# Attention and two feed-forward blocks on one core: where the moving operands of the matrix products begin in memory

## The chip, the core and the metric

The kernel runs on one core of one Trainium2 chip. The core has a matrix engine (TensorE, PE in the profile), a vector engine (DVE), an activation engine (ACT), GpSimd (POOL) and a queue engine (SP) that starts the transfers. All of them work on one on-chip memory of 128 partitions; an address in this text is a byte offset inside a partition, the same in all 128. The metric is the device time in microseconds of one execution; of three timed executions the median counts.

A matrix product on TensorE has two operands. The stationary one is loaded ahead (LDWEIGHTS, PEld in the profile), 128 columns here. The moving one is streamed past it (MATMUL), 448 or 384 columns of four bytes here.

## What is computed

The reference is a causal attention over 2 batches, 12 heads, 448 positions and 64 values a head, followed by two feed-forward blocks on the 896 tokens:

```
scores = scale * q @ k.T, masked above the diagonal
attn   = softmax(scores);  x = attn @ v             -> [896, 768]
x      = (silu(x @ w_gate) * (x @ w_val)) @ w_out    # 768 -> 1536 -> 768
h      = x @ w_in                                    # 768 -> 2048
out    = (h * clip(h + 3, 0, 6) / 6) @ w_out         # 2048 -> 768
```

## The kernel before

Every product of the two blocks is made three times at a reduced matrix type (fp32r, four bytes a value) from a value cut in two parts, high and low: high by high, high by low and low by high. So each operand is a pair of tiles, and the function `three` or `mm3_parts` issues three MATMULs for one product. Two levels of the block products are combined so that seven block products do the work of eight (`seven` and the stages after it).

The work falls into four stretches. Up to about 85 us is the attention with its transposes (`tp`, `tr`), scores (`sc`) and value products (`pv`). From there to about 429 us come the products whose moving operand has 448 columns: first layer (`x,ws`, `x,a`, `x,s`, `t,a`, `t,s`), output layer (`go,wo`, and `g8` to `g11` with `whi` and `wlo`), and the third matrix (`x,a`, `x,s` again). In the last 115 us the roles are swapped: the weights move (384 columns) and the token values are stationary; first with the gated values `h0` to `h5` as they lie (`whi` or `wlo` by `h..`), then with small tiles made for it (`op`, `tp`, `wo`).

A planner (class `Plan`) writes out the order of all instructions from a list of operations, their costs and their due times, and that order is kept. Nothing in it depends on an address.

What matters here is where the tiles lie. A "place" is a fixed stretch of the partition that a sequence of tiles uses in turn. There are 19 places in the pool `xpool` and 25 more in `ypool`. They hold tiles of [128, 2, 448] or [128, 896] four-byte values, 3,584 bytes, of either kind: plain float32 intermediates, which begin at the place's first byte, and operands of type fp32r. For the second kind the function `moving` (line 303, called from `last` at line 684 and `spot` at line 848) takes a tile of `2 * S + 8` values, 3,616 bytes, and uses the 896 values from the fourth on (`ODD = 3`), so that they begin 12 bytes into the place. The second half of such a tile (the low part, or the second batch) begins 1,792 bytes, seven times 256, after the first.

The stationary operands of the 448-column products, and both operands `op` and `wo` of the last stretch, lie in other pools: eight tiles called `ws` in `ring`, which lies ahead of `xpool`, and a ninth in `more`, which lies behind it. They begin at their first byte.

In the program as it is built, `ring` begins at byte 16,640, and every `ws` tile in it at a multiple of 256. `xpool` begins at byte 59,648, a multiple of 256 too, and its places follow one another every 3,616 bytes (3,584 where a place never holds an operand). 3,616 is 14 times 256 plus 32. So the moving operands begin 12, 44, 76, 108, 140, 172, 204 or 236 bytes past a multiple of 256, some at each. The ninth `ws` tile begins 32 bytes past a multiple of 256. The text calls this remainder, the first byte modulo 256, the offset of an operand.

```
def moving(pool_, tag, shape, name):                                    # L303
    t = pool_.tile([128, 2 * S + 8], F32R, tag=tag, name=name)[:, ODD : ODD + 2 * S]
    return t if len(shape) == 2 else t.rearrange("p (a b) -> p a b", a=2)
def spot(place, shape, dt, name):                                       # L845
    if dt == F32R and shape in ([128, 2, S], [128, NT]):
        return Spot(lambda: moving(pool_, tag, shape, name), place)
```

Of the kernel before, what the change touches and what calls it, by code (L numbers as in the profile page):

```python
# [8 lines left out]
F32 = mybir.dt.float32  # L9
BF16 = mybir.dt.bfloat16  # L10
F32R = mybir.dt.float32r
# [46 lines left out]
AT_START = {"act": 2.0, "vec": 1.3, "pool": 2.0, "pe": 1.2, "sp": 0.3}  # L58
GROUPS = ((2,), (0, 1), (3,))
IDLE = (6, 1, 3, 4)  # L60
ODD = 3
SHARED = ("vec", "pool")


# [26 lines left out]
class Plan:  # L91
# [6 lines left out]
    def op(self, where, call, reads=(), writes=(), port=False, wire=0.0, soon=None, kind=None, by=None):  # L98

        i, before, ready = len(self.ops), set(), 0.0  # L100
        for writing, spots in ((False, reads), (True, writes)):
            for s in spots:
                spot, part = s if isinstance(s, tuple) else (s, None)
                if spot not in self.uses:
                    self.uses[spot] = []
                    old = self.on_place.get(spot.place)
                    if old is not None:
                        spot.after = {j for _, j, _ in self.uses[old]}
                    if spot.place is not None:
                        self.on_place[spot.place] = spot  # L110
                before |= spot.after
                ready = max(ready, spot.ready)
                one = spot.place is not None and spot.place[0] is self.alone
                for p, j, w in self.uses[spot]:
                    if (w or writing or one) and (p is None or part is None or p == part):
                        before.add(j)
                self.uses[spot].append((part, i, writing))
        before.discard(i)
        self.ops.append((where, call, before, ready, port, wire + LANDING if wire else 0.0))
        self.soon.append(soon)  # L120
        self.kinds.append(kind)
        self.by.append(by)
# [93 lines left out]
def tile_attention_glu_mlp(  # L216
# [21 lines left out]
    B, H, S, D = q.shape  # L238
    NT, DM = out.shape
# [21 lines left out]
    consts = const.tile([128, 32], F32, name="half")  # L261
    half, floor = consts[:, :16], consts[:, 16:]
    ring = ctx.enter_context(tc.tile_pool(name="ring", bufs=1))
    xpool = ctx.enter_context(tc.tile_pool(name="xpool", bufs=1))
    banks = ctx.enter_context(tc.tile_pool(name="banks", bufs=1, space=PSUM))

# [32 lines left out]
    more = []  # L299
    lent = {}  # L300
    HD = KD // 2

    def moving(pool_, tag, shape, name):  # L303
        t = pool_.tile([128, 2 * S + 8], F32R, tag=tag, name=name)[:, ODD : ODD + 2 * S]
        return t if len(shape) == 2 else t.rearrange("p (a b) -> p a b", a=2)

    def pair_tile(name, dt=F32R):
        return slot([128, 2, S], dt, name)
# [26 lines left out]
    def attention():  # L335
        with ExitStack() as st:
# [13 lines left out]
            for i in range(NV):  # L350
                t = fix.tile([C, 2, NC, D + 16], F32, name=f"v1_{i}")
# [6 lines left out]
            def take(kind, n, shape, dt=F32, ready=0.0):  # L358

                i = count[kind] = count.get(kind, -1) + 1  # L360
                tag = f"{kind}{i % n}"
                return Spot(lambda: wk.tile(shape, dt, tag=tag, name=kind), (wk, tag), ready=ready)

            def bank(use):
                n = idle.pop(0)
                return Spot(lambda: banks.tile([128, 512], F32, tag=f"bank{n}", name=use), (banks, n)), n
# [263 lines left out]
            def pv_parts(p):  # L630

                if p < 0 or p >= NPAIR:
                    return []
                b, hp = pairs[p]
                vt, ets, sm = v_of[p], et_of.pop(p), s_of.pop(p)
                box = {}

                def product(kc):
                    if kc == 0:
                        box["o"], box["n"] = bank("pv")  # L640
                    o, w = box["o"], (NC - kc) * C

                    def work(eng):
                        for j, et in enumerate(ets):
                            eng.matmul(
                                o()[64 * j : 64 * j + 64, kc * C : S], vt()[:, j, kc, :D], et()[:, KOFF[kc] : KOFF[kc] + w],
                                start=(kc == 0), stop=(kc == NC - 1),
                            )

                    op({"pe": w * 0.0018}, work, reads=[(et, kc) for et in ets] + [vt], writes=[o], kind="pv")  # L650

                def shares():
                    r, rb = take("r", 2, [C, 2, NC]), take("rb", 1, [C, NC, 2, D])
                    tr, bn = bank("tr")
                    rs = box["rs"] = take("rs", 1, [128, S])
                    op(
                        {"pool": 0.22},
                        lambda e: e.tensor_scalar(out=r(), in0=sm(), scalar1=EPS, scalar2=None, op0=ALU.add),
                        reads=[sm], writes=[r],
                    )  # L660
                    op({"vec": 0.19}, lambda e: e.reciprocal(out=r(), in_=r()), writes=[r])
                    op(
                        {"pool": 0.72},
                        lambda e: e.tensor_copy(
                            rb(), r().rearrange("p j c -> p c j").unsqueeze(3).to_broadcast([C, NC, 2, D])
                        ),
                        reads=[r], writes=[rb], port=True,
                    )

                    def work(eng):  # L670
                        for c in range(NC):
                            eng.transpose(
                                tr()[:, c * C : (c + 1) * C], rb()[:, c].rearrange("p j d -> p (j d)"), ident[:C, :C]
                            )

                    op({"pe": 0.4}, work, reads=[rb], writes=[tr], kind="tp")
                    op({"act": 0.44}, lambda e: e.copy(rs(), tr()[:, :S]), reads=[tr], writes=[rs])
                    idle.append(bn)

                def last():  # L680
                    o, rs = box["o"], box["rs"]
                    t = sum_of[id((sums if hp < HD else more_sums)[hp % HD][0])]
                    pool_, tag = place = free.pop(0)
                    x = Spot(lambda: moving(pool_, tag, [128, 2, S], f"x{b}{hp}"), place)
                    x1[b][hp] = x
                    op(
                        {"vec": 0.52},
                        lambda e: e.tensor_tensor(out=t()[:, b], in0=o()[:, :S], in1=rs(), op=ALU.mult),
                        reads=[o, rs], writes=[(t, b)],
                    )  # L690
                    idle.append(box["n"])
                    op(
                        {"pool": 0.57, "act": 0.46}, lambda e: move(e, x()[:, 0], t()[:, b]), reads=[(t, b)],
                        writes=[(x, 0)], by=BY_END if p == NPAIR - 1 else None, port=True,
                    )
                    op(
                        {"pool": 1.16, "vec": 0.58},
                        lambda e: e.tensor_tensor(
                            out=x()[:, 1], in0=t()[:, b], in1=x()[:, 0].bitcast(F32), op=ALU.subtract
                        ),  # L700
                        reads=[(t, b), (x, 0)], writes=[(x, 1)], by=BY_END if p == NPAIR - 1 else None, port=True,
                    )
                    if b == 1 and hp < HD:
                        op(
                            {"pool": 1.16, "vec": 0.58},
                            lambda e: e.tensor_tensor(out=t()[:, 0], in0=t()[:, 1], in1=t()[:, 0], op=ALU.subtract),
                            reads=[(t, 1)], writes=[(t, 0)], port=True,
                        )

                return [lambda kc=kc: product(kc) for kc in range(2)] + [shares] + [  # L710
                    lambda kc=kc: product(kc) for kc in range(2, NC)
                ] + [last]
# [120 lines left out]
    def mlps():  # L833
# [10 lines left out]

        def spot(place, shape, dt, name):  # L845
            pool_, tag = place
            if dt == F32R and shape in ([128, 2, S], [128, NT]):
                return Spot(lambda: moving(pool_, tag, shape, name), place)
            return Spot(lambda: pool_.tile(shape, dt, tag=tag, name=name), place)

        def here(tile_and_place, ready=0.0):
# [199 lines left out]
        for h in range(HD):  # L1051
# [5 lines left out]
            for k, src in ((1, f1), (3, f3), (2, f2), (4, f4)):  # L1057
                t = take([128, 2, S], F32R, f"t{k}{h}")
# [415 lines left out]
        for eh in range(2):  # L1474
# [7 lines left out]
            for t in range(TT):  # L1482
# [4 lines left out]
                if eh == 0:  # L1487
# [3 lines left out]
                    lambda e, t=t, o=parked[t], pt=pt, eh=eh: (e.copy if t % 2 else e.tensor_copy)(  # L1491
                        o()[:, eh], eh_ap(pt())
                    ),
# [36 lines left out]
        x = [bank_spot() for _ in range(HT)]  # L1530
# [111 lines left out]
```

## Time and profile before

| what | value |
|---|---|
| median of 3 runs | 542.26 us (541.87 to 542.31) |
| the profiled execution's own time | 542.55 us |
| its span, first to last instruction | 540.8 us |
| TensorE busy | 534.3 us (99%), 3,099 MATMULs |
| VectorE / ScalarE / GpSimd busy | 455.9 / 418.6 / 146.2 us (84 / 77 / 27%) |
| granted TensorE clock | 1.000 over the span |
| transfers | 69.32 MB, mean 128 GB/s |

MATMULs overlap in the profile: each is shown with its latency, and the next begins before it ends. What a MATMUL adds to the time is the distance from its start to the start of the next one, called its spacing here. Over a run of n MATMULs the spacing is the start of what follows minus the start of the run, divided by n. Where a row of the timeline gives only a run's start and length, the last MATMUL's own length is taken off and the rest divided by n - 1.

### The profile page before, as it was taken

The numbers are of one execution on the slowest core, as the hardware profiler recorded it, in microseconds if no ns is written. First come the engines' busy times: TensorE is split into PE (matmuls) and PEld (weight loads), VectorE is DVE, ScalarE is ACT, GpSimd is POOL, SyncE is SP. The second block draws the span as 40 slices with busy tenths as digits, with TensorE's granted clock in tenths as the row PEclk, the third lists the DMA queues.
The fourth block names the chain that finished last, engine by engine and source line by source line (L and its number), as shares of the span: only waits on it lengthen the run. The fifth ranks groups of instructions, "written<-read, shape, count | busy, mean of one in ns | idle before, by whom it ended". The sixth has DMA issues, their size and how long they took to land.

```text
span 540.8 us, 8943 instructions
## 1 busy us (share of the span) xinstructions
PE 534.3 (99%) x3099; PEld 487.6 (90%) x3099; DVE 455.9 (84%) x931; ACT 418.6 (77%) x877; POOL 146.2 (27%) x163
## 2 busy tenths in 40 slices
PE   8999999999999999999999999999999999999997
PEld 4777777999999999999999999999999999999997
DVE  4999997999878778688998888989888956599982
ACT  5999996878887678588967788899898756686560
POOL 0798988403000000030030143322231300000311
PEclk9999999999999999999999999999999999999999
DMA  7987803355545443332002354465353155510112
GB/s 204 245 215 201 170 17 118 117 180 191 182 148 181 134 135 135 118 116 79 1 1 78 110 176 135 127 185 166 117 163 130 35 180 195 176 58 2 59 45 102
DMA packets 58989, 69.32 MB, mean 128 GB/s; under 512 B 16960, under 2 KB 52544, under 8 KB 58944
## 3 DMA queue, kind: packets, MB, share of 16 engines
q1 hardware_dynamic: 58944, 68.76, 42.4%
q8 instruction: 24, 0.39, 0.3%
q14 instruction: 21, 0.17, 0.1%
HBM read 65.99 MB, written 2.75 MB: 127 GB/s over the span
## 4 chain that ended last, share of the span: by engine, by line
PE 98%; DVE 1%; ACT 0%; issue 0%
PE mm L74 83%; PE pv L74 5%; PE sc L74 4%; PE tp L74 4%; PE tr L74 2%; PE zero L74 1%; DVE out L74 0%; ACT e L74 0%; DVE et L74 0%; ACT qh L74 0%; DVE e L74 0%; DVE zeros L341 0%; DVE half L840 0%; DVE half L839 0%; DVE m L74 0%
## 5 line engine op out<-in xcount | busy, mean ns | idle before, releaser
L74 PE MATMUL mm<-x,a 128*128 128x448 f32 x396 | 85.9, 363 | 0.0
L74 PE MATMUL mm<-x,s 128*128 128x448 f32 x378 | 80.6, 363 | 0.0
L74 PEld LDWEIGHTS mm<-x,a 128*128 128x128 f32 x396 | 74.6, 189 | 5.3
L74 PEld LDWEIGHTS mm<-x,s 128*128 128x128 f32 x378 | 71.2, 188 | 5.1
L74 ACT ACTIVATE raw<-raw,half 128x768 uint32<-128x768 uint8 (+1 forms) x66 | 64.5, 981 | 0.0
L74 PE MATMUL mm<-t,s 128*128 128x448 f32 x270 | 57.8, 363 | 0.0
L74 PE MATMUL mm<-op 128*128 128x384 f32 x315 | 56.5, 336 | 0.0
L74 PEld LDWEIGHTS mm<-op 128*128 128x128 f32 x315 | 55.1, 188 | 0.0
L74 PEld LDWEIGHTS mm<-t,s 128*128 128x128 f32 x270 | 50.7, 188 | 3.7
L74 PE MATMUL mm<-go,wo 128*128 128x448 f32 x252 | 51.2, 363 | 0.0
L74 PEld LDWEIGHTS mm<-go,wo 128*128 128x128 f32 x252 | 47.4, 188 | 3.5 <-issue 0.2
L74 ACT ACTIVATE e<-e,m 112x224 f32<-112x224 f32 (+3 forms) x96 | 49.7, 535 | 0.6 <-DVE m L74 0.6
L74 DVE CUSTOM_DVE_ANT_0 e<-sc,mask 112x224 f32<-112x224 f32 (+3 forms) x96 | 36.6, 440 | 1.2 <-PE sc L74 1.1
L74 DVE SCALAR_TENSOR_TENSOR v<-v,raw 128x768 uint32<-128x768 uint32 x36 | 34.3, 954 | 2.7 <-ACT raw L74 2.4
L74 ACT ACTIVATE w<-raw 128x768 f32<-128x768 f32 (+1 forms) x34 | 29.6, 870 | 8.6 <-DMA raw<-in_moe_w_out_dram 4.3
L74 ACT ACTIVATE v<-raw 128x768 f32<-128x768 f32 x36 | 32.5, 907 | 1.2 <-DMA raw<-in_moe_w_val_dram 1.0
L74 PE MATMUL mm<-x,ws 128*128 128x448 f32 x144 | 30.1, 366 | 0.0
L74 DVE SCALAR_TENSOR_TENSOR w<-w,raw 128x768 uint32<-128x768 uint32 (+1 forms) x30 | 27.2, 906 | 3.0 <-ACT raw L74 3.0
L74 PEld LDWEIGHTS mm<-x,ws 128*128 128x128 f32 x144 | 26.8, 188 | 2.2
L74 ACT COPY tmp<-mm 128x448 f32<-128x448 f32 x40 | 21.2, 532 | 9.0 <-PE mm L74 8.8
L74 ACT CAST op<-h 128x384 fp32r<-128x384 f32 x30 | 15.3, 511 | 16.2 <-PE mm L74 15.5
L74 PE MATMUL tp<-keep,e 112*112 112x112 f32 x240 | 25.8, 260 | 1.4 <-ACT e L74 1.4
(252 smaller groups left out, 1253.6 us busy)
## 6 DMA issues: line engine op xcount, KB each, us to landing
raw<-in_moe_w_out_dram SPq DMA_DIRECT2D x24, 768.0 KB, 4.2
raw<-in_moe_w_in_dram SPq DMA_DIRECT2D x16, 768.0 KB, 4.5
raw<-in_moe_w_gate_dram SPq DMA_DIRECT2D x12, 768.0 KB, 4.2
raw<-in_moe_w_val_dram SPq DMA_DIRECT2D x12, 768.0 KB, 4.2
raw<-in_moe_w_out_dram SPq DMA_DIRECT2D x6, 512.0 KB, 3.4
v<-in_v_dram SPq DMA_DIRECT2D x12, 224.0 KB, 5.1
out_dram<-out SPq DMA_DIRECT2D x14, 192.0 KB, 1.9
nat<-in_k_dram SPq DMA_DIRECT2D x10, 216.0 KB, 4.9
```

The costliest lines, as they stand in the source:

```text
L74: ins = call(*args, **kw)
```

## The change

The function `moving` and the constant `ODD` go. An operand of type fp32r takes a tile of its own size, 3,584 bytes, and begins at the place's first byte, as the plain tiles do. A pool of its own, `front`, with one tile of eight four-byte values (32 bytes) that nothing reads or writes, is put between `ring` and `xpool`.

```
-ODD = 3
+FRONT = 8
...
     ring = ctx.enter_context(tc.tile_pool(name="ring", bufs=1))
+    front = ctx.enter_context(tc.tile_pool(name="front", bufs=1))
+    front.tile([128, FRONT], F32, name="front")
     xpool = ctx.enter_context(tc.tile_pool(name="xpool", bufs=1))
...
-    def moving(pool_, tag, shape, name):
-        t = pool_.tile([128, 2 * S + 8], F32R, tag=tag, name=name)[:, ODD : ODD + 2 * S]
-        return t if len(shape) == 2 else t.rearrange("p (a b) -> p a b", a=2)
-
...
-                    x = Spot(lambda: moving(pool_, tag, [128, 2, S], f"x{b}{hp}"), place)
+                    x = Spot(lambda: pool_.tile([128, 2, S], F32R, tag=tag, name=f"x{b}{hp}"), place)
...
-            if dt == F32R and shape in ([128, 2, S], [128, NT]):
-                return Spot(lambda: moving(pool_, tag, shape, name), place)
             return Spot(lambda: pool_.tile(shape, dt, tag=tag, name=name), place)
```

All five engines have the same instructions in the same order as before; only addresses differ. In the changed program `xpool` begins at byte 59,680 and every place, in `xpool` and `ypool`, is 3,584 bytes (14 times 256) after the one before. All moving operands of the 448-column products therefore have offset 32, and so have the stationary slices of `h0` to `h5`. The `ring` tiles stay at offset 0 and the ninth `ws` tile at offset 32. The attention's own pools move by 512 bytes as a whole, so that their offsets stay, but for the identity matrix of the transposes, which lies in a place of `xpool` and goes from offset 160 to 32.

## Rows read from the trace of the kernel before

**Rows 1.** The page's chain of work that ended last, by engine and line.
```profile
PE 98%; DVE 1%; ACT 0%; issue 0%
```
**Rows 2.** That chain in order of time: start us, us, what.
```profile
92.59 443.01 PE mm L74 x2274
```
**Rows 3.** Waits of PE: engine, line, waited for: us in total, times, longest us.
```profile
PE tp L74 <- ACT e L74: 1.4, 1, 1.4
PE zero L74 <- DVE half L840: 1.2, 1, 1.2
PE sc L74 <- DVE m L74: 0.3, 1, 0.3
```
**Rows 4.** Busy us by stretch: us, PE, PEld, DVE, ACT, POOL, clock, DMA share, GB/s.
```profile
85.00:420.00 335.00, 335.00 (x1681) 311.21 (x1680) 289.43 (x495) 270.77 (x489) 69.76 (x60) 1.00 0.40 128
```
**Rows 5.** MATMUL timeline, output layer: start us, us, operation, count.
```profile
249.12 47.21 PE L74 MATMUL mm<-go,wo 128*128 128x448 f32 x233
```
**Rows 6.** MATMUL timeline, first layer, products of nine.
```profile
118.08 1.98 PE L74 MATMUL mm<-x,a 128*128 128x448 f32 x9
119.90 3.79 PE L74 MATMUL mm<-t,s 128*128 128x448 f32 x18
123.53 1.97 PE L74 MATMUL mm<-x,a 128*128 128x448 f32 x9
125.34 2.03 PE L74 MATMUL mm<-t,s 128*128 128x448 f32 x9
127.21 1.99 PE L74 MATMUL mm<-x,a 128*128 128x448 f32 x9
129.04 2.01 PE L74 MATMUL mm<-t,a 128*128 128x448 f32 x9
130.89 1.98 PE L74 MATMUL mm<-x,s 128*128 128x448 f32 x9
```
**Rows 7.** PE groups by form: operation, count, busy us, mean ns of one, idle.
```profile
L74 PE MATMUL mm<-go,wo 128*128 128x448 f32 x252 | 51.2, 363 | 0.0
L74 PE MATMUL mm<-g11l,whi 128*128 128x448 f32 x12 | 4.4, 367 | 0.0
L74 PE MATMUL mm<-g10h,whi 128*128 128x448 f32 x12 | 4.3, 360 | 0.0
```
**Rows 8.** MATMUL timeline, one round over `h2` to `h5` in the last layer.
```profile
434.56 0.34 PE L74 MATMUL mm<-whi,h2h 128*128 128x384 f32 x1
...
436.49 0.34 PE L74 MATMUL mm<-whi,h5l 128*128 128x384 f32 x1
```
**Rows 9.** By tile: count: duration ns min/median/max, first and last start us.
```profile
L74 PE MATMUL mm<-wlo,h2h x14: 332/332/336, 434.7 to 469.6; 128*128 128x384 f32 x14
...
L74 PE MATMUL mm<-wlo,h3h x14: 339/342/342, 435.3 to 470.1; 128*128 128x384 f32 x14
```
**Rows 10.** MATMUL timeline, last stretch, both operands at a tile's first byte.
```profile
485.68 10.11 PE L74 MATMUL mm<-op 128*128 128x384 f32 x57
495.63 1.21 PE L74 MATMUL mm<-op,tp 128*128 128x384 f32 x6
496.67 3.30 PE L74 MATMUL mm<-op 128*128 128x384 f32 x18
```
**Rows 11.** MATMUL timeline, attention scores, operands at a tile's first byte.
```profile
44.42 0.37 PE L74 MATMUL sc<-kh,qh 64*112 64x448 f32 x2
44.62 0.37 PE L74 MATMUL sc<-kl,qh 64*112 64x448 f32 x2
44.83 0.37 PE L74 MATMUL sc<-kh,ql 64*112 64x448 f32 x2
```
**Rows 12.** DVE and ACT groups by form that write operands or plain tiles.
```profile
L74 DVE TENSOR_TENSOR x<-tmp,x 128x448 fp32r<-128x448 f32 x9 | 5.4, 616 | 0.0
...
L74 DVE TENSOR_TENSOR ts<-g 128x448 f32<-128x448 f32 x4 | 2.5, 615 | 0.0
L74 ACT CAST go<-g 128x448 fp32r<-128x448 f32 x24 | 13.4, 566 | 7.0 <-PE mm L74 6.6
...
L74 ACT CAST qh<-f 128x448 fp32r<-128x448 f32 x3 | 1.7, 564 | 0.0
```
**Rows 13.** By tile, the attention's transposes.
```profile
L74 PE MATMUL tp<-keep,e x240: 257/259/311, 11.2 to 88.7; 112*112 112x112 f32 x120
```

## The prediction, as it was put on record

> **What bounds the kernel now.** I read the chain of work that ended last first: 98% of it is TensorE [rows 1], and from 92.59 us to 535.60 us it is one unbroken piece of 2,274 MATMULs [rows 2]. The waits say the same from the other side: TensorE's waits that have a releaser are three, 2.9 us together, all in the attention or ahead of it [rows 3]. The table by stretch shows why: from 85 to 420 us TensorE is busy for all of 335 us at clock 1.00, while VectorE has 289 us and ScalarE 271 us of work in it and the transfers fill 0.40 of their engines [rows 4]. So the time is a sum of MATMUL spacings. What an instruction of another engine costs matters only if it becomes 14% longer; what a MATMUL costs matters at once: one nanosecond on each 448-column MATMUL is 1.7 us.
>
> How long is the spacing? The run of 233 `go,wo` has a length of 47.21 us, of which the last MATMUL's own 0.36 us is no spacing: 46.85 / 232 = 201.9 ns for 448 columns [rows 5]. I take this for all 1,674 MATMULs with 448 columns (396 `x,a`, 378 `x,s`, 270 `t,s`, 252 `go,wo`, 144 `x,ws`, 90 `t,a`, and 12 groups of 12 with `g8` to `g11`). In the last layer the spacing of 384 columns is 1.93 us / 11 = 175.5 ns while the gated values `h` are stationary [rows 8], and (495.63 - 485.68) / 57 = 174.6 ns with `op` [rows 10].
>
> **Does an address matter at all?** The change moves no instruction; only where operands begin differs. Rows of equal shape that differ by nothing but the place of an operand must answer. They do. The 14 MATMULs of `wlo,h2h` last 332 to 336 ns, the 14 of `wlo,h3h`, one tile on, 339 to 342 ns, in two separate passes [rows 9]: the place decides, not chance. The same holds for the moving side: 360 ns with `g10h` and 367 ns with `g11l` as moving operand [rows 7]. The products of nine in the first layer show it as spacing, and the program tells their offsets. The `x,a` from 123.53 us has its three moving tiles at offsets 12, 44 and 76: (125.34 - 123.53) / 9 = 201.1 ns. The `x,a` from 118.08 and from 127.21 us has them at 172, 204 and 236: 202.2 and 203.3 ns. The `t,a` from 129.04 us has 140, 172 and 204: 205.6 ns [rows 6]. Stationary tiles are at offset 0 in nearly all of them. So there are good offsets and bad ones, some 3 ns apart, and before the change the kernel pays an average over them.
>
> [...]
>
> **The change part by part.** First term: all 1,674 moving operands of 448 columns come to one offset, 32, and begin at the place's first byte. Of this no row shows both together. The nearest offsets that a row shows are 12, 44 and 76, at 201.1 ns [rows 6]. Bounds: below, nothing excludes that the first byte itself costs; the shortest steady spacing of operands that all begin at a tile's first byte is 173.3 ns for 384 columns, (496.67 - 495.63) / 6, against 175.5 ns with a stationary operand 12 bytes further [rows 8, 10]. If 448 columns won the same 2.2 ns, they would have 199.7 ns. Above, the spacing of aligned operands may simply grow with the columns: 174.6 x 448 / 384 = 203.7 ns, and the attention's aligned pairs of 448 columns have (44.83 - 44.42) / 2 = 205 ns [rows 11], though these use half the rows of the array each. I take 201.1, the row that is nearest in shape and offset: 1,674 x (201.9 - 201.1) = 1.34 us less.
>
> Second term: 252 MATMULs of the last layer have a slice of `h0` to `h5` as stationary operand (18 groups of 14, as in [rows 9]). Its offsets were spread; now all are 32. Bounds: nothing, or down to 173.3 ns as above, 0.55 us. I take 174.6, the long run of aligned operands: 252 x 0.9 = 0.23 us less, call it 0.25.
>
> Third, all else at nothing. The 375 MATMULs with `op`, `tp` and `wo` keep their addresses in `ring` or their offsets in the pools behind `xpool`. VectorE and ScalarE write operands 12 bytes into a place as fast as plain tiles (616 against 615 ns, and 566 against 564 ns [rows 12]); should they become slower, the 14% of slack above hides it. Transposes now read an identity matrix at another offset; the median of the 240 is 259 ns and the shortest 257 [rows 13], over rows `e` at many offsets, so I cost them nothing; one nanosecond each would be 0.24 us. The transfers go to other pools, which keep their offsets. With TensorE 0.3% faster nothing else is late: the next limit, VectorE, is at 86% of the longest stretch.
>
> Sum: 542.55 us, the profiled execution's own time (span 540.8 and 1.75 us around it), less 1.59 gives 540.96. That execution was 0.29 us above the median of the runs, 542.26; on the median's scale the forecast is 540.7 us. The terms of its own range: 448 columns at 200.6 to 201.6 ns, 539.8 to 541.5 us.
>
> **The rivals.** A, slower: one offset for all is a bad one. Moving and weight reads then stand in the same relation in every MATMUL, where now they change from tile to tile and the bad relations are averaged with good ones. For it speaks that the aligned runs are the dearer ones per column: 174.6 / 384 = 0.455 ns against 201.9 / 448 = 0.451 [rows 5, 10], and the 205 ns of the attention [rows 11]; against it, that the bad offsets seen are 140 to 236 and not those around 32 [rows 6]. Price: 203.7 ns, 1,674 x 1.8 = 3.0 us more, 0.25 less, so 545.0 us. It decides from about 202.7 ns on, where 1,674 x 0.8 passes 1.1 us and the second term together.
>
> B, no change: offset and first byte even out, the spacing stays at 201.9, and only the second term is left: 542.0 us. For it speaks that the products of nine differ by little around their mean; that offsets 12 to 76 are the good ones rests on few rows.
>
> C, much faster: the first byte costs by itself. [...] At 2.2 ns as above: 1,674 x 2.2 + 252 x 2.2 = 4.2 us, 538.0 us. For it speaks the 173.3 ns run, against it that 448 columns at 12 bytes are no dearer per column than 384 at none. [...]
>
> **How the numbers follow.** The forecast has 0.42, C 0.12, B 0.27, A 0.19. A measurement of this kernel tells 0.2%, about 1.1 us, from no change. Of the forecast's 0.42, 0.06 is within that, since its range ends at 541.5 and the bound is 541.2. So faster is 0.36 + 0.12 = 0.48, the same 0.27 + 0.06 = 0.33, slower 0.19. The range for 8 in 10 cuts off the far part of C and most of A: 538.4 to 543.6 us; the forecast's own is 539.8 to 541.5.
>
> **What would show it.** In the profile after, `go,wo` should have about 46.7 us for 232 spacings, the products of nine should be equal within 0.5 ns instead of 201 to 206, the groups of `g8` to `g11` should have one mean, near 362 ns, instead of 360 to 367, and the 18 groups of `h` one median near 335. If they become equal but at 364 ns or more, A is right; equal at 363, B; near 360, C. If they stay apart, then the offset modulo 256 is not what the place decides by, and the argument is wrong. A gain with unchanged spacings, or a wait of TensorE on VectorE or ScalarE that is not there now, would make it wrong too.

## The result and the profile after

The changed kernel takes 548.99 us (median of four executions, 548.79 to 549.29) against 542.24 us before (541.87 to 542.31): a ratio of 1.0126, interval 1.0109 to 1.0144. It is 6.75 us slower. The forecast was 540.7 us, within 538.4 to 543.6; slower had a chance of 0.19, and the rival that spoke of it had 545.0 us.

The profiled execution after took 549.13 us with a span of 547.3 us at clock 1.000. The chain of waits (start us, us, what) shows at once where the time is; it answers to [rows 2]:

```profile
92.01 450.16 PE mm L74 x2274
```

The same unbroken piece of 2,274 MATMULs is 7.15 us longer. It begins 0.58 us earlier; together that is the 6.6 us between the two profiled executions. Nothing waits that did not wait before. TensorE's waits after (engine, line, waited for: us in total, times, longest us), as in [rows 3]:

```profile
PE tp L74 <- ACT e L74: 1.4, 1, 1.4
PE zero L74 <- DVE half L838: 1.2, 1, 1.2
PE sc L74 <- DVE m L74: 0.3, 1, 0.3
```

The table by stretch (us, PE, PEld, DVE, ACT, POOL, clock, DMA share, GB/s) for the same 335 us as [rows 4]:

```profile
85.00:420.00 335.00, 335.00 (x1642) 303.78 (x1641) 284.01 (x484) 265.34 (x478) 67.79 (x58) 1.00 0.40 125
```

TensorE is busy all the time at full clock, as before, but 1,642 MATMULs fit where 1,681 did: 1681 / 1642 = 1.024 times the spacing. A busy share of 100% hides that. VectorE and ScalarE did a little less in the stretch, into which less of the program falls.

The output layer in the MATMUL timeline (start us, us, operation, count), against [rows 5]:

```profile
252.09 48.26 PE L74 MATMUL mm<-go,wo 128*128 128x448 f32 x233
```

(48.26 - 0.37) / 232 = 206.4 ns where there were 201.9. Over 1,674 MATMULs 4.5 ns are 7.5 us: the whole loss and a little more. The products of nine, against [rows 6]:

```profile
118.07 2.02 PE L74 MATMUL mm<-x,a 128*128 128x448 f32 x9
...
123.64 2.02 PE L74 MATMUL mm<-x,a 128*128 128x448 f32 x9
125.60 2.11 PE L74 MATMUL mm<-t,s 128*128 128x448 f32 x9
127.54 2.00 PE L74 MATMUL mm<-x,a 128*128 128x448 f32 x9
129.38 2.07 PE L74 MATMUL mm<-t,a 128*128 128x448 f32 x9
131.29 2.00 PE L74 MATMUL mm<-x,s 128*128 128x448 f32 x9
...
214.91 2.02 PE L74 MATMUL mm<-x,a 128*128 128x448 f32 x9
216.77 2.02 PE L74 MATMUL mm<-t,s 128*128 128x448 f32 x9
218.63 2.02 PE L74 MATMUL mm<-x,a 128*128 128x448 f32 x9
220.49 2.02 PE L74 MATMUL mm<-t,a 128*128 128x448 f32 x9
```

The `x,a` that had the good offsets, from 123.64 us, has gone from 201.1 to (125.60 - 123.64) / 9 = 217.8 ns with a gap of some 0.1 us in it. A few gaps lie in this stretch, and between two of them the next `x,a` has (129.38 - 127.54) / 9 = 204.4 ns. Later, as in the rows from 214.91 us, every nine has 1.86 us, whatever its operands, and the starts of single MATMULs follow one another at 206, 207, 207 ns, over and over. The mean of that pattern, 206.7 ns, is met again below. By form (operation, count, busy us, mean ns of one, idle), against [rows 7]:

```profile
L74 PE MATMUL mm<-go,wo 128*128 128x448 f32 x252 | 52.3, 369 | 0.0
L74 PE MATMUL mm<-g11l,whi 128*128 128x448 f32 x12 | 4.4, 369 | 0.0
L74 PE MATMUL mm<-g10h,whi 128*128 128x448 f32 x12 | 4.4, 368 | 0.0
```

The 360 and the 367 have become equal but for a nanosecond, and both long. By tile (count: duration ns min/median/max, first and last start us), the two groups of the last layer [rows 9] have become equal too; the `op` of the last stretch is wanted further below:

```profile
L74 PE MATMUL mm<-wlo,h2h x14: 336/336/336, 441.8 to 476.2; 128*128 128x384 f32 x14
L74 PE MATMUL mm<-wlo,h3h x14: 336/336/336, 442.3 to 476.7; 128*128 128x384 f32 x14
...
L74 PE MATMUL mm<-op x315: 332/334/346, 478.1 to 542.9; 128*128 128x384 f32 x158
```

And the last stretch, whose offsets did not change, takes what it took [rows 10]:

```profile
509.52 26.87 PE L74 MATMUL mm<-op 128*128 128x384 f32 x153
536.23 1.21 PE L74 MATMUL mm<-op,tp 128*128 128x384 f32 x6
```

(536.23 - 509.52) / 153 = 174.6 ns. So the loss lies in the 448-column MATMULs alone: from the recorded starts, without the few gaps over 230 ns, 201.87 ns before and 206.41 after. What is left to explain is why.

### The profile page after: what moved, and what is told of

The parts are those of the page before. It is cut to its first block, busy times and chain, and to the rows that moved or that the text cites. A ratio compares the mean times of both kernels' runs of the same rounds, so it can differ in the third digit from the quotient of the medians.

```text
span 547.3 us, 8942 instructions
## 1 busy us (share of the span) xinstructions
PE 540.8 (99%) x3098; PEld 486.0 (89%) x3099; DVE 456.0 (83%) x931; ACT 419.5 (77%) x877; POOL 146.8 (27%) x163
## 4 chain that ended last, share of the span: by engine, by line
PE 98%; DVE 1%; ACT 0%; issue 0%
PE mm L74 83%; PE pv L74 5%; PE sc L74 4%; PE tp L74 4%; PE tr L74 2%; PE zero L74 1%; DVE out L74 0%; ACT e L74 0%; DVE et L74 0%; ACT qh L74 0%; DVE e L74 0%; DVE zeros L339 0%; DVE half L838 0%; DVE half L837 0%; DVE m L74 0%
## 5 line engine op out<-in xcount | busy, mean ns | idle before, releaser
L74 PE MATMUL mm<-x,a 128*128 128x448 f32 x396 | 87.8, 369 | 0.0
L74 PE MATMUL mm<-x,s 128*128 128x448 f32 x378 | 82.4, 369 | 0.0
L74 PE MATMUL mm<-t,s 128*128 128x448 f32 x270 | 59.1, 369 | 0.0
L74 PE MATMUL mm<-go,wo 128*128 128x448 f32 x252 | 52.3, 369 | 0.0
L74 DVE TENSOR_TENSOR tmp<-mm,tmp 128x448 f32<-128x448 f32 x30 | 18.5, 621 | 11.1 <-PE mm L74 10.8
```

The source lines that it names most:

```text
L74: ins = call(*args, **kw)
```

## The experiments

The change does two things to a moving operand at once: its first byte goes from 12 bytes into a place to 0, and all operands come to one offset. The theories at the outset were that the offset 32 is a bad one (P in the expectations), that the lost 12 bytes cost (F), and that equality itself costs (K). The 16 bytes that the expectations count first bytes by are an assumption: no run shows a unit of that size. The kernels skew12, skew16 and one0 to one12 multiply other columns than the reference wants, and kick leaves columns out; they are there for the time alone. Times are medians beside the kernel before on the same chip; spacings are means over the recorded starts of 448-column MATMULs without gaps over 230 ns.

**odd0: the kernel before, without its 12 bytes.** The offsets stay spread (0, 32, 64 ...).

```
-ODD = 3
+ODD = 0
```

> The kernel before with its places of 3,616 bytes, 32 bytes past a multiple of 256 from one to the next, but the moving operands begin at the place's first byte: aligned as after, at offsets spread over eight values as before. Theory F (the first byte itself: an operand that begins 12 bytes past a multiple of 16 is streamed faster than one that begins at a multiple of 16): spacing of 448 columns 206 to 207 ns as after, 548 to 549 us. Theory K (one common offset for all operands is what costs, whatever the first byte): spacing near 201.9 ns, 542 us less the 0.3 us of the last layer at most. Theory P (only the particular offset 32 is a bad one): an average, 202 to 204 ns, 542 to 545 us.

544.19 us against 542.55: 1.0038 (1.0025 to 1.0051), 203.0 ns. The output layer in its timeline:

```profile
249.15 47.72 PE L74 MATMUL mm<-go,wo 128*128 128x448 f32 x234
```

(47.72 - 0.36) / 233 = 203.3 ns. The 12 bytes alone are worth 1.6 us of the 6.75. That is near the 203.7 ns that rival A had for aligned operands; the rest came only with the common offset 32. The mean hides a spread by offset, from the recorded starts and the offsets of the built program: the 260 MATMULs of odd0 at offset 32 have 204.3 ns, the most of its eight offsets, and the 283 at 64 have 201.5 ns, the least. Of the three theories only P had a range that held 203.0 ns.

**skew12: the changed kernel, each 448-column MATMUL reading its tile 12 bytes late or 4 early.**

```
+    def skew(t, i):
+        flat = t if len(t.shape) == 2 else t.rearrange("p a b -> p (a b)")
+        at = i * S + (3, -1)[i]
+        return flat[:, at : at + S]
...
-      [(a()[:, 0, k], a()[:, 1, k], x()[:, 0], x()[:, 1]) for k, x in enumerate(xk)],
+      [(a()[:, 0, k], a()[:, 1, k], skew(x(), 0), skew(x(), 1)) for k, x in enumerate(xk)],
```

> The changed kernel with all its addresses, but each MATMUL of 448 columns reads its moving operand from 12 bytes behind the first half's first byte, or from 4 bytes ahead of the second half's, so that every read begins 12 bytes past a multiple of 16, at offset 44 or 28. It multiplies shifted columns: the output is not the reference's, the work is the same. F: 201 to 202 ns, 541 to 542.5 us. K: 206 ns, 548 to 549 us. P: offsets 44 and 28 lie at 32, so 206 ns, 548 to 549 us.

541.03 us, 0.9979 (0.9969 to 0.9988) of before, 201.2 ns. With the places as in the changed kernel, but the moving operands at offsets 44 and 28, the loss is gone, and 1.5 us more:

```profile
248.18 47.33 PE L74 MATMUL mm<-go,wo 128*128 128x448 f32 x234
```

**front0 and front32: the changed kernel with all moving operands at offset 0, or at 128.** At 0 the stationary operands have offset 0 too, all of them; in the changed kernel and in front32 the tiles of `ring` stay at 0. The tile in `front` is left out, or has 128 bytes.

```
-FRONT = 8
+FRONT = 32
```

> The changed kernel without the 32 bytes in front of the pool: all operands of 448 columns, moving and stationary, at offset 0. F: 206 to 207 ns, 548 to 549 us. K: the same 206 to 207 ns. P: another offset, so another spacing, 201 to 204 ns, 541 to 545 us.

> The changed kernel with 128 bytes in front of the pool instead of 32: all moving operands of 448 columns at offset 128, stationary ones at 0. F: 206 to 207 ns, 548 to 549 us. K: the same. P: another spacing than 206.4 ns by 2 ns or more, so another time by 3 us or more.

front32 took 546.0 us, 1.0066 (1.0051 to 1.0081), 203.9 ns, with starts that repeat 209, 196, 203, 212, 200. So one common aligned offset can cost more or less: 32 isn't the only dear one, but it is the dearest of the three. A spacing other than 206.4 ns was what P had foreseen for both, and it came out for front32 and for most executions of front0; F and K had 206 to 207. front0 has times that one would not take for those of one program: ten executions from 541.80 to 548.33 us, median 542.75 (1.0015, 0.9991 to 1.0038), where the twenty of the kernel before lay between 541.86 and 543.46. The profiled one was the longest. Up to 124 us its spacings are 202.7 ns (199, 207, 202, 203, 203, over and over); after one gap of 0.77 us they are 206.7 to the end of the 448 columns. Its output layer:

```profile
251.68 48.52 PE L73 MATMUL mm<-go,wo 128*128 128x448 f32 x234
```

**front0_again: the same program, one more execution.**

> The kernel without the 32 bytes in front once more, the same program as before, for a second profile. Theory L (equal aligned addresses allow more than one repeating pattern, and what came before in the same execution chooses): stretches at 206.7 ns and stretches at 200 to 203 ns, another share of each than the first profile had, and a time anywhere from 541.8 to 548.4 us. If addresses alone decide: 206.7 ns from 125 us on as in the first profile, and 548.3 us.

542.89 us. Every address is the same, and the spacing is 202.7 ns nearly throughout; the pattern 206, 207, 207 appears only between two gaps, from 125.6 to 128.9 us:

```profile
249.70 47.60 PE L73 MATMUL mm<-go,wo 128*128 128x448 f32 x234
```

48.52 against 47.60 us for the same 234 instructions at the same addresses, at clocks of 1.000 and 0.999. The two are from different chips, but the ten executions of front0 are from one, all at 1.000, and lie up to 6.5 us apart. So addresses alone do not set the spacing. This stream of equal MATMULs settles into a repeating pattern, and in front0 which one it is changed at a gap, of 0.77 us.

**one0, one8, one12: the changed kernel with every 448-column MATMUL at one single address within its place, 0, 8 or 12 bytes in (offsets 32, 40 or 44).** The function is that of skew12 with another line:

```
+        at = 0      # one0
+        at = 2      # one8
+        at = 3      # one12
```

> The changed kernel, but each MATMUL of 448 columns reads the first half of its moving tile, in place of the second half too (the output is not the reference's, the work is the same): one offset, 32, as in the changed kernel. All theories: spacing 206 to 207 ns in a repeating 207, 206, 207, and 548 to 549.5 us. If it is not, the two halves differ in some way that the offset modulo 256 does not tell.

> As the run before, from the third value on: one common offset, 40, 8 bytes past a multiple of 16. F, if what counts is to begin inside a 16-byte stretch: as with 12 bytes, 201 to 202.5 ns; F, if 8 bytes count as aligned: 206 to 207 ns. K: 206 to 207 ns, 548 to 549 us.

> As the run before, with the first half read from its fourth value on (shifted columns, so the output is not the reference's): one common offset, 44, that begins 12 bytes past a multiple of 16. Theory F (the first byte decides): 201 to 202.5 ns, 541 to 543 us. Theory K (a common offset locks the spacing at its bad value; the run with offsets 44 and 28 was faster only because two offsets alternate): 206 to 207 ns, 548 to 549 us.

549.48 us for one0 (1.0125, 1.0095 to 1.0154), 541.18 for one8 (0.997, 0.9955 to 0.9985) and 541.83 for one12 (0.9983, 0.9972 to 0.9994). Spacings 206.3, 200.8 and 201.5 ns. One common first byte is no loss by itself; one common first byte at offset 32, 0 bytes into the place, is the whole loss. The output layers of one8 and of one12:

```profile
248.97 47.30 PE L74 MATMUL mm<-go,wo 128*128 128x448 f32 x234
```

```profile
248.71 47.38 PE L74 MATMUL mm<-go,wo 128*128 128x448 f32 x234
```

The place of the other operand counts as well. In one8 every moving operand has offset 40, and the first group of these rows has the ninth `ws` tile (offset 32) as its stationary operand, the second a tile at offset 0:

```profile
151.37 2.02 PE L74 MATMUL mm<-t,s 128*128 128x448 f32 x9
153.23 1.96 PE L74 MATMUL mm<-x,a 128*128 128x448 f32 x9
155.03 1.96 PE L74 MATMUL mm<-t,a 128*128 128x448 f32 x9
```

(153.23 - 151.37) / 9 = 206.7 ns and (155.03 - 153.23) / 9 = 200.0 ns; over the whole run 205.7 for the 176 MATMULs with the ninth tile and 200.3 for the others.

one0 shows the pattern changing inside one execution. Its timeline has these two groups `x,s` with the same kind of operands, moving at offset 32 and stationary at 0:

```profile
131.29 1.97 PE L74 MATMUL mm<-x,s 128*128 128x448 f32 x9
133.09 3.84 PE L74 MATMUL mm<-t,s 128*128 128x448 f32 x18
...
157.22 2.02 PE L74 MATMUL mm<-x,s 128*128 128x448 f32 x9
159.08 3.88 PE L74 MATMUL mm<-t,s 128*128 128x448 f32 x18
```

(133.09 - 131.29) / 9 = 200.0 ns in the first and (159.08 - 157.22) / 9 = 206.7 ns in the second and in nearly all others. The 200.0 ns begin behind a gap of 314 ns at 125.55 us and outlast another at 129.06. They end at 133.09 us without a gap: there nine MATMULs with the ninth `ws` tile begin, and behind these the spacing is 206.7 again. In the changed kernel too the spacing of 204.4 ns behind the gaps ends at that tile, at 133.1 us.

**skew16: as skew12, with 16 bytes or none, so that neighbours alternate between offsets 48 and 32.**

```
+        at = i * S + (4, 0)[i]
```

> The changed kernel with the first half read from its fifth value on and the second half as it is (shifted columns, so the output is not the reference's): two offsets that alternate, 48 and 32, 16 bytes apart as 44 and 28 were, both multiples of 16. F: 205 to 207 ns, 547 to 549 us. K: alternation breaks the pattern, 201 to 203 ns, 541 to 544 us.

546.12 us, 1.0061 (1.0038 to 1.0083), 204.4 ns. Two aligned offsets in turn give back under half of the loss; the same alternation 4 bytes lower (skew12) gives back all. Neither F nor K had this: F said 205 to 207 ns, K 201 to 203. From the starts, the MATMULs at offset 32 still have 207.3 ns, those at 48 have 202.9: the gain lies with the operands that left offset 32.

**ws8: the changed kernel with the stationary `ws` tiles 8 bytes into places of 3,104 bytes.** If only the relation between the reads of the two operands counted, this should be one8 again with the sides exchanged. The wider places also spread the offsets of the `ws` tiles in steps of 32 and push the places of `ypool` on, so that 906 of the 1,674 moving operands begin at offset 64 and 768 at 32.

```
+    def late(pool_, tag, shape, name):
...
+        t = pool_.tile([128, 776], F32R, tag=tag, name=name)[:, 2 : 2 + n]
```

> The changed kernel, but the stationary tiles called ws begin 8 bytes into their places (which take 3,104 bytes instead of 3,072, so that their offsets are spread over 8, 40, 72 and so on). Moving operands of 448 columns still begin at a multiple of 16, at offset 32 or 64. The result is the reference's. Theory M (only the moving operand's first byte counts): the spacing stays at 203 to 207 ns, 544 to 549 us. Theory R (what counts is how the two operands that are read at the same time stand to each other modulo 16): 200 to 202.5 ns, 540 to 543 us. In the last stretch op also moves 8 bytes in, both as moving and as stationary operand: where 384 columns go from 173.4 to 174.6 ns now, M expects a change if an aligned start costs there too, down to 172 ns.

545.42 us, 1.0051 (1.0036 to 1.0066). The 448-column spacing falls to 203.4 ns, two thirds of the way, the time half the way, and the last stretch, where both operands are such tiles, becomes longer. By tile:

```profile
L74 PE MATMUL mm<-op x315: 332/338/349, 474.5 to 540.0; 128*128 128x384 f32 x158
```

The median was 334 in the changed kernel. That the two operands stand 8 bytes apart, modulo 16, is not enough: it does not give the 200.8 ns of one8, and theory R failed. M's range held. What gave back the half isn't shown, since three things changed at once: the weights' first byte, the spread of their offsets, and the moving operands at 64. In the last stretch the change costs.

**odd2: the kernel before, 8 bytes into a place instead of 12.** one8 was the fastest of the single offsets; with spread ones it should be as good, if the position inside 16 bytes were all.

```
-ODD = 3
+ODD = 2
```

> The kernel before with the operands 8 bytes into their places instead of 12: offsets spread over 8, 40, 72 and so on. The result is the reference's. If to begin inside a 16-byte stretch is all that counts, as with 12 bytes: 201.9 ns, 541.5 to 543 us. If 8 bytes are better than 12, as one common offset of 40 was than one of 44: 200 to 201.5 ns, 539 to 541.5 us. If the spread offsets hit the 209 ns that offset 40 showed with the ninth ws tile: 203 ns or more, 544 us or more.

548.13 us, 1.0099 (1.0082 to 1.0116), 205.6 ns, nearly as slow as the changed kernel:

```profile
251.32 48.22 PE L74 MATMUL mm<-go,wo 128*128 128x448 f32 x234
```

For offset 40 with the ninth `ws` tile, where its expectation has 209 ns, one8 shows 205.7 ns in the mean of 176 MATMULs. A guess that failed, and it stays unexplained: 8 bytes is the best of three at one offset and the worst of three with spread ones. It also bounds what may be said of the changed kernel: odd2 has moving operands that are neither aligned nor at a common offset, and loses 5.4 us.

**kick: the changed kernel with 270 of the 1,674 MATMULs shortened to 440 columns.** No address changes; only the equality of the stream is broken.

```
+                n = S - 8 if i % 9 == 1 else S
...
+                if n == 1 and pt.shape[1] == S:
+                    pt_, rhs = pt[:, : S - 8], rhs[:, : S - 8]
```

> The changed kernel, all at offset 32 or 0 as there, but 270 of the 1,674 MATMULs (one in nine, in the output layer one in three) stream 440 columns instead of 448, so that eight sums in each such product lack one of their three parts and the output is not the reference's. [...] Theory L (equal MATMULs in a row fall into a repeating 206, 207, 207 that an irregular one can break): 448 columns at 201 to 205 ns, 541 to 546 us. If the addresses alone decide: 206.4 ns for the other 1,404, 547.5 to 548.5 us.

543.78 us, 1.0021 (1.0012 to 1.003) of before: 5.2 us less than the changed kernel. The work left out is worth 270 x 8 columns x 206.4 / 448 = 1.0 us. The untouched MATMULs of 448 columns went from 206.4 to 203.1 ns; in this stretch of the timeline every one, long or short, stands 200 ns from the next:

```profile
297.64 0.36 PE L74 MATMUL mm<-g8h,whi 128*128 128x448 f32 x1
297.84 0.36 PE L74 MATMUL mm<-g8l,whi 128*128 128x440 f32 x1
298.04 0.36 PE L74 MATMUL mm<-g8h,wlo 128*128 128x448 f32 x1
298.24 0.36 PE L74 MATMUL mm<-g9h,whi 128*128 128x448 f32 x1
```

**good: the kernel before with eight places 32 values (128 bytes) wider, so that most operands have offsets 12, 44, 76 or 236.** This keeps the 12 bytes and the offsets that [rows 6] showed as good, and adds 236: the prediction counted it among the bad ones, but from the starts of the whole run before it has 201.1 ns, no more than 44 and 76.

```
+PADDED = ("s3", "s8", "s12", "s16", "y9", "y14", "y15", "y16")
...
+        wide = 2 * S + (40 if tag in PADDED else 8)
+        t = pool_.tile([128, wide], F32R, tag=tag, name=name)[:, ODD : ODD + 2 * S]
```

> The kernel before with its first bytes 12 bytes into the places, but eight places are 128 bytes longer, so that the moving operands of 448 columns begin at offsets 12, 44, 76 and 236 (48 of 1,674 at 108 and 140) instead of all eight. The result is the reference's. If the offsets that the trace of before showed as good ones stay good when they are the only ones: 201.2 ns instead of 201.9, 1.1 us less, 541.1 to 542 us beside a kernel before at 542.3 to 542.7. If the spacing depends on the sequence of offsets and not on each alone: anywhere from 200.5 to 203 ns, 540.5 to 544 us.

541.74 us against 542.47: 0.9984 (0.9973 to 0.9994), 201.1 ns. It leaves nothing out, and it is ahead of both kernels, of the one before by 0.7 us:

```profile
248.14 47.30 PE L75 MATMUL mm<-go,wo 128*128 128x448 f32 x234
```

Four kernels take apart what the change mixed up; the common offset is 44 in one12 and 32 in the changed kernel:

| time, spacing of 448 columns | 12 bytes in | 0 bytes in |
|---|---|---|
| offsets spread | before: 542.2 us, 201.9 ns | odd0: 544.2 us, 203.0 ns |
| one offset | one12: 541.8 us, 201.5 ns | after: 549.0 us, 206.4 ns |

Taking the 12 bytes away costs 1.6 us, bringing all to one offset costs nothing, and both together, at offset 32, cost 6.75. At other offsets the two together cost less: 546.0 us at 128 (front32), and 542.75 at 0 in the median of front0. And odd2 lost 5.4 us with neither. So the table holds for its four cells and is no rule; that offset 32 itself is a bad one, theory P, is not refuted.

## Why the prediction was wrong

What bounds the kernel was right: one sum of spacings, no wait before or after, no other engine late. That the place of an operand shows in the spacing was right too: the same instructions with other addresses differ by 6.75 us here.

The step that failed is the first term, and in it the sentence "I take 201.1, the row that is nearest in shape and offset". It was near in shape and in the offset modulo 256, but not in the first byte. That row came from operands 12 bytes into a place, among neighbours with other offsets; the change puts every operand at its place's first byte and at one offset. Good bears the row out for the kernel that it came from: with the 12 bytes kept, offsets 12, 44, 76 and 236 have 201.1 ns. It did not carry over to a stream of equal aligned MATMULs at offset 32, which had 206.4: instead of -1.34 us the term was +7.5. The bad rows were read too coarsely: the 205.6 ns of the `t,a` contain one start 217 ns from the next, and within the two `x,a` the operands at 236 have 201 ns.

The bounds failed with it. The upper one, 203.7 to 205 ns, was the nearer one. The prediction says that no row shows offset 32 and the first byte together, but the scores [rows 11] do: 448 columns, aligned, and in the program as built the moving operands of all three pairs begin at offset 32. Their 205 ns was within 1.4 of the outcome. I set them aside because they use half the rows of the array each (64*112 in their form, 128*128 in that of the others). The lower bound had the sign of the first byte the other way round.

Rival A had the direction and came nearest: one offset for all was a bad one. Its reason, that equal MATMULs stand in one relation and nothing averages it out, holds in part only: kick breaks the equality and wins most back, but one8 and one12 have one relation nearly throughout without a loss, and odd2 has spread ones at 205.6 ns. It was also too cheap. Its 203.7 ns is nearly what alignment costs with spread offsets (odd0, 203.0); the equal MATMULs at offset 32 cost 3.4 ns more. Its mark, groups that become equal at 364 ns or more, came out: 369.

Rival C had the wrong sign for this change. With all else equal, 12 bytes into a place is 7.65 us faster than 0 (one12 against one0); with spread offsets 8 bytes is 3.9 us slower than 0 (odd2 against odd0), so neither sign is a rule here. Rival B is out: the spacing moved.

The second term had the right sign and was too small. Among the 252 MATMULs with a slice of `h0` to `h5` the spacing fell from 176.2 to 173.9 ns, 0.59 us, where 0.25 was taken and 0.55 was the bound; the 175.5 ns of [rows 8] are one round, below the mean of all. That these operands became aligned and equal does not explain it by itself: in front32 they are both, at offset 128, and have 176.1 ns.

The third term held: waits, the last stretch [rows 10] and the slack of VectorE are as they were. The 0.58 us that the long piece begins earlier are not the identity matrix. The transposes had 259 ns in the median before [rows 13] and have it after, and they already start 0.5 us earlier; in kick, which has the changed kernel's addresses, they start later than in either. The first row is of the changed kernel, the two others are of kick:

```profile
L74 PE MATMUL tp<-keep,e x240: 257/259/308, 10.7 to 88.1; 112*112 112x112 f32 x120
```

```profile
L74 PE MATMUL tp<-keep,e x240: 257/259/309, 11.7 to 89.1; 112*112 112x112 f32 x120
...
93.07 444.10 PE mm L74 x2274
```

So these 0.58 us are scatter of the start.

Shown is that the loss comes from where the moving operands begin (one8 and one12 against one0 change nothing else and win all of it back), that it is a repeating pattern of the stream which equal operands at equal addresses can have or not have (front0 twice, one0 inside one execution), and that breaking the equality of the lengths takes most of it away (kick, 3.3 of the 4.5 ns). Not shown is what inside the chip makes the patterns, what chooses among them, whether the offset 32 counts for itself or stands for aligned common offsets, and why 8 bytes is best in one8 and worst in odd2.

## What to carry over

Where a kernel is a sum of MATMUL spacings, the first bytes of the operands are a parameter, worth 1.5% here between the fastest and the slowest of these kernels (skew12, 541.03 us, and one0, 549.48), and it is tried on the chip rather than tidied: a few values of the offset and of the step between places, with the spacings read from the starts. A row from a mixed stream doesn't price a uniform one (201.1 ns here, where 206.4 came); when a change alters two properties at once, look for the row that has both, however different it is otherwise, and let it set the range. Where operands are aligned and equal, compare several executions before a difference of 1% is believed: those of front0 lay up to 1.2% apart.

## What the runs showed of the hardware

MATMULs of 448 columns, each with its weight load, at full clock, have several steady spacings that repeat over long stretches: 200.0 ns (one8, stretches of one0 and kick), 202.7 (front0: 199, 207, 202, 203, 203), 204.0 (front32: 209, 196, 203, 212, 200) and 206.7 (after: 206, 207, 207). With all moving operands at one offset, the MATMULs with the ninth `ws` tile as stationary operand had 205.7 ns, the others 200.3 (one8). TensorE's busy share shows none of it: it was busy for all of the 335 us both before and after. One program, front0, took 541.80 to 548.33 us in ten executions at clock 1.000. The profiled one, 548.33 us, had 206.7 ns to the end of the 448 columns after a gap at 124 us; that of front0_again, 542.89 us at clock 0.999, had 202.7 nearly throughout.
